# Pooled attention and a routed feed-forward in one program: another order of issue for the attention part, and the reordering of the second static block's columns moved behind the last attention unit

## The chip, the cores and the metric

The kernel runs on one core of one Trainium2 chip. The metric is the device time of one execution in microseconds (us). Of the kernel before, three runs took 790.5, 791.36 and 796.12 us (median 791.36). The engines are called by their short names: PE (TensorE: matmuls and transposes), DVE (VectorE), ACT (ScalarE), POOL (GpSimd), and SP, which here only starts transfers (DMA).

## The reference

Attention with keys and values that are averaged over groups of 8 rows, then a feed-forward layer in which each token goes through one of 8 experts. The token's choice can depend on its forerunner: where a local gate is closed, it keeps the expert of the token before.

```python
B, H, S, D = 8, 8, 576, 64            # pool = 8, so 72 pooled keys per head
k_p = k.reshape(B, H, 72, 8, D).mean(axis=3);  v_p = v.reshape(B, H, 72, 8, D).mean(axis=3)
attn = softmax(q @ k_p.T / sqrt(D));           x = (attn @ v_p), heads side by side: [B, S, 512]
for b, s:                              # E = 8 experts, F = 1024
    fresh = argmax(x[b, s] @ w_gate)
    e = fresh if s == 0 or sigmoid(x[b, s] @ w_local) < 0.5 else the e of s - 1
    out[b, s] = softmax(x[b, s] @ w_gate)[e] * (relu(x[b, s] @ w1[e]) @ w2[e])
```

## The kernel before

The program has three parts. **Attention** (0 to some 233 us of the span): the 8 batch entries go in pairs; a pair has five units of query rows, so there are 20 units (unit 5*pair + t; t = 4 is the last rows of both entries, "stacked"). **Static blocks**: after two pairs the most used expert is chosen, its weights are loaded, and two blocks of 256 of its tokens are run through it by code without branches. **Blocks**: a loop over a table that the kernel computes runs all the remaining tokens, 256 at a time, and changes experts as the table says.

Attention and static blocks are written as steps, and nothing but hand-written lists of step names (PLAN, PLAN_B, PLAN_C, lines 54 to 99) sets the order in which the steps are issued: `run(plan)` calls `do(name, n)` (line 758), which issues that step's instructions to the engines' queues. Each engine then works through its own queue in that order and waits, instruction by instruction, for what it needs; nothing overtakes. The names:

- `lv`, `lk`, `lq`: SP starts the load of a tile of values, keys, queries. `lc`, `pf`: loads of the gate weights and prefill of the token lists.
- values (prep_v, line 408): `vp` pools a tile (POOL, or DVE with `.d`), `vt` transposes it (PE), `vc` copies it (ACT), `vl` multiplies it by the gate weights (PE), `vd` puts that into the table `vaug` (DVE, line 436), `vm` (place_v, line 439) puts the pooled values into `vaug` (line 444; POOL, or DVE with `.d`). `kp` pools keys (DVE).
- a unit n: `sc` scores (PE), `mx` row maxima (DVE, line 490), `sb` subtract (DVE, line 493), `ex` exponentials (ACT), `T0` to `T2` transposes (PE, line 524) with their copies `T0c` to `T2c` (ACT, tile aT), `v0` to `v2` products with the values (PE, line 566) with their copies (ACT, tile osb), `fs` sums and gate logits (DVE, line 583 on), `fp` and `fd` the two halves of the output rows (POOL and DVE, line 603; `.p`: both on POOL) and their store (SP).
- a pair: `rA`, `rT0` to `rP` the routing of its tokens, a chain over DVE, PE and ACT; then nine times `s`: POOL scatters token numbers into the lists `ids`.
- the chosen expert: `ch`, `er` choose it; `w1`, `w2` (SP) load its weights, 4 tiles each; `p1`, `p2` split a tile into a high and a low part: a cast on ACT (tile w1h or w2h), then a subtraction on POOL (lines 213, 218).
- a static block n: `il` (line 257) loads its token numbers from `ids` (SP, line 259, four transfers); `ga` (line 262) sums them on DVE (lines 263, 264) and gathers the rows on POOL (two transfers, line 270); `XR` (line 279) puts the gathered rows' columns in another order: two copies on ACT (line 281); `X0`, `X1` transpose them (PE, line 288) and split them (ACT, DVE). `L1`, `h0`, `h1`, `L2` are the columns of its two matrix products: `h0` is line 337 (ACT) and 338 (DVE). Three PSUM tiles hp hold the columns of the first product.

```python
    elif op == "ga":
        xgs[n] = ld.tile([P, 2, D], F32, name="qt", bufs=4)
        rows_gather(n, xgs[n], 4 * S)
    elif op == "XR":
        xgs[n], src = ld.tile([P, 2, D], F32, name="qt", bufs=4), xgs[n]
        rows_order(src, xgs[n])
    elif op == "p1":
        split1(first1[n], n, nc.vector if arg else nc.gpsimd)

def split1(src, c, eng):
    nc.scalar.copy(out=W1[0][:, c, :], in_=src)
    eng.tensor_tensor(out=W1[1][:, c, :], in0=src, in1=W1[0][:, c, :].bitcast(F32), op=ALU.subtract)
```

Of the kernel before, what the change touches and what calls it, by code (L numbers as in the profile page):

```python
# [59 lines left out]
T1:1 lv:9 kp:6 lk:8 T1c:1 T2:1 v2:2 T2c:1 sc:3 v2c:2 lk:9 fs:2 v0:1 lq:7 mx:3 fp:2 v0c:1 v1:1 fd.p:2 sb:3 vp:8 v1c:1  # L60
v2:1 sc:4 v2c:1 ex:3 fs:1 vt:6 lq:8 vt:8 mx:4 fp:1 vc:6 vc:8 T0:3 sb:4 vm:8 fd:1 vm:6 T0c:3 T1:3 kp:7 vp:7 T1c:3
T2:3 vl:6 T2c:3 sc:5 vd:6 ex:4 lk:10 T0:4 mx:5 vp:9 lv:10 lv:11 lq:9 T0c:4 T1:4 vl:8 T1c:4 vt:7 vd:8 sb:5 vc:7 v0:3
vm:7 lv:12 kp:8 v0c:3 v1:3 ex:5 lk:11 v2:3 v1c:3 vl:7 v2c:3 v0:4 fs:3 v0c:4 v1:4 vd:7 fp:3 T0:5 v1c:4 fs:4 fd.p:3
T0c:5 T1:5 rA:0 fp:4 T1c:5 T2:5 sc:6 fd.p:4 T2c:5 vp:11 vt:9 lq:10 mx:6 vt:11 vc:9 vl:9 vc:11 vm:11 rT0:0 vm:9 vd:9
# [24 lines left out]
""")
# [1130 lines left out]
```

## Time and profile before

| | us |
|---|---|
| three runs | 790.5, 791.36, 796.12 |
| the profiled execution | 789.34 |
| its span, from the first to the last instruction | 786.9 |
| attention, up to the first product of a static block | 233.6 |
| static blocks and the first of the table's, up to about | 300 |
| busy: PE, DVE, ACT, POOL | 657.8, 450.9, 273.8, 437.8 |
| mean granted clock of PE, as a share of full speed | 0.899 |

The profiled execution is 2.0 us below the median of the three runs. Times in rows count from the span's start. In a timeline a row is a run of like instructions: start, busy time, engine, line, operation, output <- input, count, and in brackets the idle time in front of it and what ended that.

### The profile page before, as it was taken

What the parts mean: (1) busy time and instruction counts of PE and PEld (TensorE: products, weight loads), DVE (VectorE), ACT (ScalarE), POOL (GpSimd) and SP (SyncE); (2) the same over time, 40 slices, a digit from 0 to 9 for tenths busy, and PEclk for the clock granted to TensorE, in tenths of its full rate; (3) what the DMA queues carried; (4) which work ended last, traced back from release to release, by engine and by line L of the source; (5) the groups of instructions that cost most, each with busy time, mean ns of one, the idle gap of its engine ahead of it and who ended that gap; (6) DMA issues with size and microseconds to landing.
All of it is one profiled execution on the core that took longest, in us unless ns stands there. A gap on an engine that the chain in (4) does not pass through costs nothing. (4 is left out here: it accounts for less than half of the span.)

```text
span 786.9 us, 14972 instructions
## 1 busy us (share of the span) xinstructions
PE 657.8 (84%) x3588; PEld 545.8 (69%) x3589; DVE 450.9 (57%) x1058; ACT 273.8 (35%) x613; POOL 437.8 (56%) x659
## 2 busy tenths in 40 slices
PE   2878989966687999799999799789979996999980
PEld 2767878855685788577878676568868774877860
DVE  4696758797276635233478237387824386633450
ACT  1244434433543323122164125165512165321130
POOL 5156766573664543456546556556656556646443
PEclk9998779866798999899999899899989997999995
DMA  7897745452312162111116116225711146411110
GB/s 236 284 317 248 234 174 180 146 202 54 122 54 67 31 203 106 44 41 42 42 56 242 52 36 213 83 91 197 256 54 35 42 132 223 176 50 42 42 41 29
DMA packets 49377, 96.77 MB, mean 123 GB/s; under 512 B 22974, under 2 KB 22978, under 8 KB 49348
## 3 DMA queue, kind: packets, MB, share of 16 engines
q1 hardware_dynamic: 38820, 74.34, 28.1%
q0 software_dynamic: 10528, 22.08, 8.7%
q8 instruction: 14, 0.23, 0.1%
q14 instruction: 15, 0.12, 0.0%
HBM read 76.28 MB, written 22.21 MB: 125 GB/s over the span
## 5 line engine op out<-in xcount | busy, mean ns | idle before, releaser
L314 POOL DMA_INDIRECT kt<-x_rows,idk x168 | 180.1, 1072 | 49.7 <-issue 43.4
L330 PE MATMUL hp<-x,w1h 128*128 128x512 f32 x376 | 147.1, 426 | 11.7 <-ACT w1h L212 5.0
L351 PE MATMUL o_ps<-w2h,ht_h 128*128 128x512 f32 x312 | 123.9, 397 | 2.7 <-PEq L1140 1.0
L351 PE MATMUL o_ps<-w2l,ht_h 128*128 128x512 f32 x312 | 122.8, 394 | 0.0
L351 PE MATMUL o_ps<-w2h,ht_l 128*128 128x512 f32 x312 | 122.8, 394 | 0.0
L332 PE MATMUL hp<-x,w1l 128*128 128x256 f32 x376 | 112.4, 299 | 8.0 <-DVE w1l L213 3.1
L330 PEld LDWEIGHTS hp<-x,w1h 128*128 128x128 f32 x376 | 76.5, 204 | 32.5 <-issue 11.2
L338 DVE TENSOR_TENSOR hs<-hp,hs 128x256 f32<-128x256 f32 x94 | 39.2, 423 | 100.1 <-ACT hs L337 66.3
L337 ACT COPY hs<-hp 128x256 f32<-128x256 f32 x94 | 34.3, 367 | 165.3 <-PE hp L332 46.1
L332 PEld LDWEIGHTS hp<-x,w1l 128*128 128x128 f32 x376 | 76.8, 204 | 13.4 <-issue 12.7
L566 PE MATMUL op<-vaug,aT 128*128 128x148 f32 (+4 forms) x448 | 75.4, 346 | 4.1 <-ACT aT L376 4.0
L566 PEld LDWEIGHTS op<-vaug,aT 128*128 128x128 f32 (+1 forms) x448 | 69.3, 208 | 9.5 <-ACT aT L376 5.2
L351 PEld LDWEIGHTS o_ps<-w2h,ht_h 128*128 128x128 f32 x312 | 59.5, 191 | 16.9 <-issue 4.5
L342 ACT ACTIVATE ht_h<-hs 128x256 fp32r<-128x256 f32 x136 | 57.0, 419 | 35.4 <-DVE hs L338 21.3
L351 PEld LDWEIGHTS o_ps<-w2h,ht_l 128*128 128x128 f32 x312 | 59.3, 190 | 12.8 <-DVE ht_l L343 0.2
L351 PEld LDWEIGHTS o_ps<-w2l,ht_h 128*128 128x128 f32 x312 | 59.5, 191 | 11.7
L1065 DVE TENSOR_SCALAR ob<-o_ps,m_a 128x512 f32<-128x512 f32 x42 | 31.4, 749 | 59.1 <-PE hp L332 16.2
L343 DVE SCALAR_TENSOR_TENSOR ht_l<-hs,ht_h 128x256 fp32r<-128x256 f32 x136 | 57.0, 419 | 8.0 <-ACT ht_h L342 7.1
L1086 POOL TENSOR_TENSOR kt<-idk,zf 128x8 f32<-128x8 f32 x20 | 8.6, 432 | 90.4 <-DVE idk L305 86.5
L1076 POOL DMA_INDIRECT out<-ob,m_e x42 | 44.8, 1067 | 25.0 <-issue 25.0
L702 POOL DMA_INDIRECT ids<-pm,pos x36 | 35.5, 988 | 19.1 <-DVE pos L699 9.4
L323 ACT CAST x<-qt 128x512 fp32r<-128x512 f32 x40 | 22.8, 618 | 60.3 <-DVE qt L318 60.3
(265 smaller groups left out, 1199.5 us busy)
## 6 DMA issues: line engine op xcount, KB each, us to landing
raw<-in_moe_w SPq DMA_DIRECT2D x56, 512.0 KB
kk<-in_k SPq DMA_DIRECT2D x16, 576.0 KB
vt_in<-in_v SPq DMA_DIRECT2D x16, 512.0 KB
...
```

The costliest lines, as they stand in the source:

```text
L314: nc.gpsimd.indirect_dma_start(out=xk[:, j, :], out_offset=None, in_=x_pc[0:4 * rows], in_offset=bass.IndirectOffsetOnAxis(ap=idk[:, j:j + ...
L330: nc.tensor.matmul(out=ps, lhsT=W1[0][:, kk, f * P:(f + 1) * P], rhs=xt[:, kk].rearrange("p i n -> p (i n)"), start=(kk == 0), stop=False, ...
L332: nc.tensor.matmul(out=ps[:, 0:2 * P], lhsT=W1[1][:, kk, f * P:(f + 1) * P], rhs=xt[:, kk, 0, :], start=False, stop=(kk == KD - 1), skip_g ...
L337: nc.scalar.copy(out=hb[:, 0, :], in_=ps[:, 2 * P:])
L338: nc.vector.tensor_tensor(out=hb[:, 1, :], in0=ps[:, 0:2 * P], in1=hb[:, 0, :], op=ALU.add)
L342: nc.scalar.activation(out=ht[0][:, f, :], in_=hb, func=AF.Relu)
L343: nc.vector.scalar_tensor_tensor(out=ht[1][:, f, :], in0=hb, scalar=0.0, in1=ht[0][:, f, :].bitcast(F32), op0=ALU.max, op1=ALU.subtract)
L351: nc.tensor.matmul(out=to[h], lhsT=ht[i][:, kk, h * P:(h + 1) * P], rhs=W2[j][:, kk, :], start=(n == 0), stop=(n == 3 * KF - 1))
L566: nc.tensor.matmul(out=out, lhsT=lhs, rhs=rhs if len(out.shape) == 3 else rhs.rearrange("p s x -> p (s x)"), start=all(x[0] != n for x in ...
L702: nc.gpsimd.indirect_dma_start(out=ids[u % 4].rearrange("t m w -> (t m) w"), out_offset=bass.IndirectOffsetOnAxis(ap=pos[:, u:u + 1], axis=0),
L1065: nc.vector.tensor_scalar(out=ob[:, h, :], in0=o_ps[h], scalar1=m_a[:, h, 1:2], scalar2=None, op0=ALU.mult)
L1076: nc.gpsimd.indirect_dma_start(out=outv, out_offset=bass.IndirectOffsetOnAxis(ap=m_e[h][:, 0:1], axis=0), in_=ob[:, h, :], in_offset=None, ...
```

## The change

The list of steps of the attention part is replaced by another list of the same steps, and one step leaves it: `XR:1`, the reordering of the second static block's columns, which stood at the end of PLAN, now stands in PLAN_B behind `rO:3`, a late step of the last pair's routing, and ahead of `L1:4`, the fifth column of the first static block. A few steps change engine: DVE places values (`vm.d`) of tiles 3, 5, 8, 9, 14, 18, 19, 20, 21 and 22 where it was 0, 4, 16, 18, 19, 20 and 23 (16 instructions of line 444 where there were 12), and pools (`vp.d`) tiles 2 and 23 where it was 3. The loop and the products of the static blocks stay as they are. PLAN_C is the same. One line more in the list shifts all line numbers behind it by one (444 is 445 after, and so on). From the lists, of some 34 lines each:

```diff
@@ PLAN
...
-s:0 p1:3 T1:15 rA:2 T0c:15 sc:16 T1c:15 T2:15 vt:21 T2c:15 mx:16 s:0 vt:23 vc:21 vl:21 vc:23 rT0:2 s:0 vd:21 sb:16
-vl:23 fp:13 rT1:2 il:0 il:1 vd:23 ex:16 vm.d:23 fp:14 sc:17 fd:13 vm:21 fd:14 rS0:2 T0:16 rS1:2 ga:0 XR:0 T0c:16
...
+T0:14 s:0 v0c:13 sb:15 v1:13 T0c:14 il:0 il:1 p1:0 T1:14 vp.d:23 v2:13 T1c:14 v1c:13 vl:19 v2c:13 vt:21 vd:19 ex:15
...
@@ PLAN_B
 rA:3 L1:0 h0:0 h1:0 L1:1 h0:1 L1:2 rT0:3 rS0:3 h1:1 rT1:3 h0:2 rS1:3 h1:2 L1:3 rT2:3 rE:3 rS2:3 h0:3 h1:3 rL:3 rO:3
-L1:4 rR:3 ct:0 rV:3 rP:3 h0:4 h1:4 s:0 s:0 s:0 s:0 s:0 s:0 s:0 s:0 s:0 L1:5 tc:0 cn:0 i1:0 h0:5 h1:5
+XR:1 L1:4 rR:3 ct:0 rV:3 rP:3 h0:4 h1:4 s:0 s:0 s:0 s:0 s:0 s:0 s:0 s:0 s:0 L1:5 tc:0 cn:0 i1:0 h0:5 h1:5
...
```

**First place: the weight splits on POOL and the placing of values on DVE.** POOL's queue before, from the fourth of the second pair's nine scatters (L702) on; w1l and w2l are splits of weight tiles:

```order
L702 DMA ids3_67<-pm_1704,pos_1721 65536x2
L702 DMA ids0_64<-pm_1704,pos_1721 65536x2
L702 DMA ids1_65<-pm_1704,pos_1721 65536x2
L213 TENSOR_TENSOR w1l_154<-kt_1791,w1h_153 128x1024
L218 TENSOR_TENSOR w2l_156<-vt_in_1793,w2h_155 128x1024
L213 TENSOR_TENSOR w1l_154<-kt_1795,w1h_153 128x1024
L213 TENSOR_TENSOR w1l_154<-kt_1849,w1h_153 128x1024
L702 DMA ids2_66<-pm_1704,pos_1721 65536x2
L213 TENSOR_TENSOR w1l_154<-kt_1890,w1h_153 128x1024
L702 DMA ids3_67<-pm_1704,pos_1721 65536x2
L702 DMA ids0_64<-pm_1704,pos_1721 65536x2
```

After, from the sixth scatter on (lines are one higher; xs_1821 and xs_1947 are the output rows of units 12 and 13, vaug3<-vs_1896 places value tile 23):

```order
L703 DMA ids1_65<-pm_1660,pos_1677 65536x2
L604 TENSOR_TENSOR xs_1821<-osb_1688,rr_1793 128x512
L703 DMA ids2_66<-pm_1660,pos_1677 65536x2
L703 DMA ids3_67<-pm_1660,pos_1677 65536x2
L703 DMA ids0_64<-pm_1660,pos_1677 65536x2
L214 TENSOR_TENSOR w1l_154<-kt_1799,w1h_153 128x1024
L445 TENSOR_TENSOR vaug3_210<-vs_1896,mk_97 128x2x64
L604 TENSOR_TENSOR xs_1947<-osb_1856,rr_1917 128x512
L214 TENSOR_TENSOR w1l_154<-kt_1801,w1h_153 128x1024
L219 TENSOR_TENSOR w2l_156<-vt_in_1791,w2h_155 128x1024
L267 MEMSET qt_2027 128x1024
L271 DMA qt_2027<-x_rows_63,idr0_191 128x512 x2
```

All nine scatters now stand ahead of the first split, and the gather of the first static block (L271) stands between the third split and the last two of w1. DVE's queue before, where the values of tiles 20, 18 and 19 are placed (L444), up to the row maxima of unit 15:

```order
L436 TENSOR_TENSOR vaug2_209<-rt_1839,mk_97 128x2x9
L436 TENSOR_TENSOR vaug2_209<-rt_1839,mk_97 128x3x9
L444 TENSOR_TENSOR vaug2_209<-vs_1549,mk_97 128x2x64
L444 TENSOR_TENSOR vaug2_209<-vs_1448,mk_97 128x2x64
L444 TENSOR_TENSOR vaug2_209<-vs_1448,mk_97 128x3x64
L444 TENSOR_TENSOR vaug2_209<-vs_1558,mk_97 128x3x64 x2
L490 TENSOR_REDUCE mx_1883<-sp_1856 128x12
L490 TENSOR_REDUCE mx_1883<-sp_1856 128x4
```

After, from the last table entries in front of the same placing (L445) to the subtraction of unit 15:

```order
L437 TENSOR_TENSOR vaug2_209<-rt_1808,mk_97 128x3x9
L445 TENSOR_TENSOR vaug2_209<-vs_1593,mk_97 128x2x64
L445 TENSOR_TENSOR vaug2_209<-vs_1519,mk_97 128x2x64
L445 TENSOR_TENSOR vaug2_209<-vs_1519,mk_97 128x3x64
L437 TENSOR_TENSOR vaug2_209<-rt_1825,mk_97 128x2x9
L604 TENSOR_TENSOR xs_1821<-osb_1688,rr_1793 128x512
L445 TENSOR_TENSOR vaug2_209<-vs_1612,mk_97 128x3x64 x2
L491 TENSOR_REDUCE mx_1862<-sp_1829 128x12
L491 TENSOR_REDUCE mx_1862<-sp_1829 128x4
L494 TENSOR_TENSOR ap_1863<-sp_1829,mx_1862 128x864
L494 TENSOR_TENSOR ap_1863<-sp_1829,mx_1862 128x288
```

The same five placing instructions now have the table entries and output rows of unit 12 among them; in the step list no `p1` or `p2` stands ahead of them.

**Second place: the first reordering on ACT.** ACT's queue before, from the exponentials of unit 16 (at_1999) to the first exponentials of unit 17; brow is the third pair's routing, aT_2041 holds transposes of unit 16, osb_2110 products of unit 15, and L281 is `XR:0`:

```order
L508 ACTIVATE at_1999<-ap_1998 128x2x80
L508 ACTIVATE at_1999<-ap_1998 128x128
L648 COPY brow_2077<-tp_2067 2x256
L281 COPY qt_2090<-qt_2080 128x4x4x32 x2
L376 COPY aT_2041<-tp_2072 128x512
L376 COPY aT_2041<-tp_2094 128x512
L376 COPY aT_2041<-tp_2105 128x128
L376 COPY osb_2110<-op_2111 128x444
L508 ACTIVATE at_2101<-ap_2100 128x2x2x216
```

After, where L282 is `XR:0`, from the exponentials of unit 16 (at_1958) to the routing copies (brow) of the third pair; osb_2042 holds products of unit 15, aT_2018 transposes of unit 16, w1h is the cast of a weight tile:

```order
L509 ACTIVATE at_1958<-ap_1957 128x2x80
L509 ACTIVATE at_1958<-ap_1957 128x128
L213 CAST w1h_153<-kt_1941 128x1024
L377 COPY osb_2042<-op_2043 128x444
L213 CAST w1h_153<-kt_1992 128x1024
L377 COPY aT_2018<-tp_2066 128x512
L377 COPY osb_2042<-op_2074 128x444
L282 COPY qt_2091<-qt_2027 128x4x4x32 x2
L377 COPY osb_2042<-op_2094 128x2x148
L377 COPY aT_2018<-tp_2080 128x512
L649 COPY brow_2111<-tp_2099 2x256
L649 COPY brow_2131<-tp_2119 2x256
```

Between the gather's issue and `XR:0` ACT now has two casts of w1 tiles, two copies of products (osb) and one of transposes (aT), where `XR:0` stood right behind `ga:0` in the list.

**Third place: the second reordering on ACT.** ACT's queue before, from the copies of unit 19's transposes and products on; L281 is `XR:1`, the rows hs<-hp and ht_h<-hs belong to the first static block's columns:

```order
L376 COPY osb_2399<-op_2400 128x444
L376 COPY osb_2399<-op_2411 128x148
L281 COPY qt_2429<-qt_2419 128x4x4x32 x2
L337 COPY hs_2466<-hp0_2477 128x256
L342 ACTIVATE ht_h_2461<-hs_2466 128x256
L337 COPY hs_2466<-hp1_2478 128x256
L648 COPY brow_2543<-tp_2538 2x256
L342 ACTIVATE ht_h_2461<-hs_2466 128x256
```

After, from the high part of the first column (L343; unit 19's copies stand ahead of it) to the reordering (L282):

```order
L343 ACTIVATE ht_h_2455<-hs_2460 128x256
L338 COPY hs_2460<-hp1_2472 128x256
L649 COPY brow_2537<-tp_2532 2x256
L343 ACTIVATE ht_h_2455<-hs_2460 128x256
L338 COPY hs_2460<-hp2_2473 128x256
L649 COPY brow_2549<-tp_2542 2x256
L343 ACTIVATE ht_h_2455<-hs_2460 128x256
L649 COPY brow_2565<-tp_2562 2x128
L655 ACTIVATE pe_2568<-sh_2485 128x72
L338 COPY hs_2460<-hp0_2471 128x256
L343 ACTIVATE ht_h_2455<-hs_2460 128x256
L282 COPY qt_2586<-qt_2394 128x4x4x32 x2
```

The first four columns and the routing copies of the last pair (brow, pe) now stand ahead of the reordering; before, only unit 19's copies did.

On SP, before, the loads of all four w1 tiles stand ahead of the eight transfers of `il:0` and `il:1`, and three of w2 behind; after, two of w1 and one of w2 stand ahead, two of w1 and three of w2 behind.

## Rows read from the trace of the kernel before

**Rows 1.** Busy time by stage: PE, PEld, DVE, ACT, POOL; granted clock, DMA share, GB/s

```profile
0.00:110.00 110.00, 82.46 (x618) 71.99 (x619) 74.84 (x177) 37.39 (x93) 59.48 (x120) 0.89 0.76 252
...
150.00:200.00 50.00, 34.52 (x237) 27.90 (x236) 40.78 (x79) 17.00 (x36) 31.66 (x29) 0.67 0.38 125
200.00:233.60 33.60, 28.04 (x225) 25.62 (x225) 17.66 (x48) 18.70 (x41) 19.72 (x17) 0.83 0.20 72
233.60:300.00 66.40, 60.81 (x315) 49.52 (x312) 36.09 (x144) 21.41 (x56) 31.40 (x38) 0.95 0.35 113
300.00:786.90 486.90, 418.16 (x1919) 340.69 (x1917) 250.51 (x531) 160.78 (x341) 269.65 (x424) 0.92 0.28 92
```

**Rows 2.** DVE, row maxima (two instructions a unit, one if stacked) in two stretches

```profile
110.50:145.00 34.50, 5.01 (x8) 0.95 0.59 196
145.00:229.00 84.00, 8.52 (x12) 0.72 0.33 113
```

**Rows 3.** What PE waited for, 150 to 245 us: total us, times, longest

```profile
PE rt L428 <- DVE vaug L436: 7.1, 2, 4.6
PE tp L524 <- ACT aT L376: 6.6, 2, 5.9
PE tp L645 <- DVE ab L630: 3.3, 1, 3.3
...
PE hp L330 <- DVE hs L338: 1.7, 1, 1.7
```

**Rows 4.** Timeline of DVE, 149 to 240 us

```profile
163.22 10.90 DVE L444 TENSOR_TENSOR vaug<-vs,mk 128x128 f32<-128x128 f32 x5
174.05 1.41 DVE L490 TENSOR_REDUCE mx<-sp 128x12 f32<-128x864 f32 x2
...
180.45 1.69 DVE L622 TENSOR_TENSOR sh<-lg,ml 128x72 f32<-128x72 f32 x1
...
183.81 2.67 DVE L635 SCALAR_TENSOR_TENSOR ab<-bm,ac,nbm 128x2 f32<-128x2 f32 x1
...
216.80 2.12 DVE L586 TENSOR_TENSOR lgx<-osb,rr 128x144 f32<-128x144 f32 x1
```

**Rows 5.** Line 444, placing on DVE: ns min/median/max, first and last start

```profile
L444 DVE TENSOR_TENSOR vaug<-vs,mk x12: 268/376/7654, 18.1 to 190.4; 128x192 f32<-128x192 f32 x8, 128x128 f32<-128x128 f32 x4
```

**Rows 6.** Timeline of POOL, 0 to 235 us

```profile
163.95 2.36 POOL L213 TENSOR_TENSOR w1l<-kt,w1h 128x1024 fp32r<-128x1024 f32 x1
...
168.57 2.34 POOL L213 TENSOR_TENSOR w1l<-kt,w1h 128x1024 fp32r<-128x1024 f32 x1
...
197.14 1.09 POOL L270 DMA_INDIRECT qt<-x_rows,idr  x1 [9.32 <-DVE idr L264]
```

**Rows 7.** Timeline of PE, 150 to 245 us

```profile
164.24 2.84 PE L467 MATMUL sp<-kd,qt 64*128 64x72 f32 x24
...
203.15 0.48 PE L524 MATMUL tp<-ident,at 128*128 128x128 f32 x1 [5.93 <-ACT aT L376]
203.41 5.54 PE L566 MATMUL op<-vaug,aT 128*128 128x148 f32 x22
...
210.40 3.40 PE L566 MATMUL op<-vaug,aT 128*128 128x148 f32 x22
```

**Rows 8.** Timeline of ACT, 0 to 235 us

```profile
201.06 0.62 ACT L281 COPY qt<-qt 128x512 f32<-128x512 f32 x1 [5.79 <-DMA qt<-x_rows,idr]
```

**Rows 9.** Timeline of ACT, 229 to 246 us

```profile
241.97 0.62 ACT L281 COPY qt<-qt 128x512 f32<-128x512 f32 x1 [4.54 <-DMA qt<-x_rows,idr]
...
243.83 0.37 ACT L337 COPY hs<-hp 128x256 f32<-128x256 f32 x1
```

**Rows 10.** What SP waited for, 150 to 245 us

```profile
SPq L259 <- DMA ids<-pm,pos: 13.9, 1, 13.9
```

**Rows 11.** Timeline of SP, 145 to 262 us

```profile
185.88 6.54 SPq L259 DMA_DIRECT2D idn<-ids  x8
```

**Rows 12.** Line 444 on DVE, 150 to 233.6 us: count, busy us, mean ns

```profile
L444 DVE TENSOR_TENSOR vaug<-vs,mk 128x128 f32<-128x128 f32 (+1 forms) x6 | 11.2, 1915 | 0.0
```

More of the change, by code (lines that the diff above doesn't have):

```diff
@@ L60 @@
[L60 to L64, printed above, removed]
@@ new lines @@
+vc:2 vm:2 vp:1 lk:3 kp:1 lv:4 vt:1 lv:5 kp:2 vm:1 lk:4 sc:0 lk:5 vl:0 mx:0 lq:4 vc:1 vd:0 sb:0 vl:2 vd:2 ex:0 vl:1
+sc:2 vd:1 T0:0 mx:2 T0c:0 T1:0 vp:3 sb:2 v0:0 T1c:0 T2:0 kp:3 v1:0 v0c:0 T2c:0 lv:6 vt:3 v1c:0 v2:0 vm.d:3 vp:5
+vc:3 lk:6 vl:3 v2c:0 sc:1 vp:4 ex:2 vd:3 fs:0 vt:5 lq:5 lq:6 T0:2 mx:1 vc:5 fp:0 lv:7 lv:8 vt:4 vl:5 vm.d:5 vc:4
+vm:4 T0c:2 vd:5 kp:4 vl:4 fd.p:0 T1:2 vd:4 vp:6 v0:2 kp:5 lk:7 T1c:2 T2:2 v0c:2 v1:2 T2c:2 kp:6 lv:9 lk:8 v1c:2
+v2:2 sb:1 lk:9 vt:6 v2c:2 vm:6 fs:2 ex:1 sc:3 fp:2 vc:6 mx:3 lq:7 T0:1 vp:8 T1:1 T0c:1 sb:3 fd.p:2 v0:1 T1c:1 vp:7
@@ new lines @@
+T2:1 kp:7 v1:1 v0c:1 T2c:1 ex:3 v2:1 vp:9 lv:10 lv:11 lk:10 v1c:1 sc:4 v2c:1 T0:3 lq:8 fs:1 vl:6 lv:12 T0c:3 T1:3
+vd:6 vt:8 fp:1 mx:4 T1c:3 vm.d:8 vc:8 sb:4 T2:3 fd.p:1 vt:7 T2c:3 kp:8 vl:8 vc:7 sc:5 vm:7 ex:4 vd:8 kp:9 lk:11
+v0:3 lq:10 T0:4 v0c:3 mx:5 vp:11 lk:12 v1:3 T0c:4 vp:10 T1:4 sb:5 v1c:3 v2:3 T1c:4 vl:7 v2c:3 vt:9 vd:7 ex:5 vt:11
+fs:3 sc:6 lv:14 lv:13 vm:11 vc:11 vm.d:9 vc:9 fp:3 vl:11 lq:9 mx:6 T0:5 vt:10 fd.p:3 T0c:5 vd:11 v0:4 kp:10 vc:10
+vm:10 T1:5 v0c:4 sb:6 vp:12 lk:14 v1:4 T1c:5 kp:11 vl:9 v1c:4 T2:5 sc:7 T2c:5 ex:6 lv:15 fs:4 vt:12 lq:11 lk:13
@@ new lines @@
+T0:6 vd:9 fp:4 rA:0 vl:10 T0c:6 fd.p:4 vm:12 vc:12 T1:6 vp:14 T1c:6 T2:6 vp:13 T2c:6 lv:16 vd:10 v0:5 mx:7 rT0:0
+v0c:5 sb:7 lv:17 v1:5 rS0:0 vp:15 rT1:0 v1c:5 ex:7 v2:5 rS1:0 rT2:0 v2c:5 sc:8 lv:18 rS2:0 fs:5 rE:0 rL:0 lq:12
+mx:8 fp:5 T0:7 v0:6 rO:0 fd.p:5 T0c:7 sb:8 rR:0 v0c:6 vp:17 v1:6 rV:0 T1:7 v1c:6 rP:0 v2:6 T1c:7 T2:7 sc:9 v2c:6
+s:0 T2c:7 ex:8 fs:6 vl:12 vt:14 s:0 v0:7 mx:9 vc:14 fp:6 vd:12 T0:8 sb:9 v0c:7 s:0 v1:7 fd:6 T0c:8 vm.d:14 kp:12
+s:0 T1:8 v1c:7 v2:7 s:0 kp:13 T1c:8 lk:15 T2:8 vl:14 s:0 T2c:8 vt:13 v2c:7 sc:10 ex:9 fs:7 s:0 vc:13 v0:8 lq:13
@@ new lines @@
+lq:14 vd:14 mx:10 fp:7 T0:9 v0c:8 s:0 fd:7 v1:8 T0c:9 sb:10 s:0 T1:9 vl:13 v1c:8 v2:8 vm:13 T1c:9 vd:13 ex:10 kp:15
+vt:15 vt:17 sc:11 vm:17 v2c:8 vm:15 vc:15 fs:8 vc:17 v0:9 lq:15 vl:15 mx:11 v0c:9 v1:9 fp:8 T0:10 vd:15 v1c:9
+fd.p:8 sb:11 T0c:10 T1:10 fs:9 T1c:10 T2:10 sc:12 T2c:10 ex:11 rA:1 fp:9 fd.p:9 vl:17 vp:16 lq:16 T0:11 v0:10
+T0c:11 vd:17 lv:19 vt:16 mx:12 lv:20 v0c:10 v1:10 vm:16 vc:16 vl:16 vp:18 sb:12 v1c:10 v2:10 rT0:1 v2c:10 vd:16
+fs:10 rT1:1 lv:21 sc:13 rS0:1 fp:10 rS1:1 rT2:1 lq:17 fd.p:10 v0:11 rS2:1 vp:20 mx:13 T1:11 v0c:11 rE:1 vp:19 kp:14
@@ L89 @@
+X0c:0 fs:16 v0:17 T1c:17 fp:16 v0c:17 v1:17 rP:2 T2:17 fd:16 sc:19 v1c:17 s:0 T2c:17 ex:18 mx:19 v2:17 s:0 v2c:17
+s:0 T0:18 sb:19 fs:17 T0c:18 s:0 v0:18 fp:17 T1:18 s:0 v0c:18 fd:17 T2:18 T1c:18 s:0 T2c:18 ex:19 v1:18 s:0 T0:19
+v1c:18 s:0 v2:18 T0c:19 T1:19 s:0 v2c:18 ga:1 v0:19 T1c:19 fs:18 v0c:19 v1:19 fp:18 v1c:19 fs:19 fd.p:18 fp:19
+fd:19 ma:0
 """)
```

37 lines of the change are left out of this document (10 added, 27 removed).

## The prediction

> **What bounds the kernel now.** I read the busy times by stage first, then the row maxima, which mark when a unit begins, then PE's waits, and last the timelines around the places where PE waited. From 300 us on the loop keeps PE busy for 418.16 of 486.9 us [rows 1]. The edit does not touch it, so it is carried over as it is. Up to 110 us PE has 82.46 us of work and the DMA engines are busy for a share of 0.76: two limits close together. Between 150 and 200 us nothing is full: PE 34.52 of 50 us, DVE 40.78, POOL 31.66, and the granted clock is 0.67 of full, between the two levels of 1.2 and 2.4 GHz. So there the order of issue and the waits decide. The row maxima say it in units: four units begin in the 34.5 us from 110.5 on, 8.6 us each, at a mean clock of 0.95. In the 84 us from 145 on it is six more, 14 us each, at 0.72 [rows 2]. Most of the list's changes that can matter are in this slow stretch.
>
> PE's waits there are for table entries of the values (7.1 us in two), for transposes that ACT has to copy (6.6, of which 5.9 in one), for the routing (3.3), and at the first static block's columns for DVE (1.7) [rows 3]. I follow two of them back.
>
> The first goes to DVE. From 163.22 us on five placing instructions take 10.90 us [rows 4], though the median of line 444 is 0.376 us; its longest took 7.654 [rows 5]. The weight splits on POOL begin at 163.95, the first of four that follow each other; that at 168.57 is the third, each takes 2.3 us [rows 6]. DVE's slow stretch lies on POOL's. Behind it on DVE stand the row maxima of unit 15. PE's scores for them began at 164.24 and took 2.84 [rows 7], so they were there at 167.08; the maxima began at 174.05 [rows 4]: 7.0 us late for DVE alone.
>
> The second goes to ACT. `XR:0` waited 5.79 us for the gather from 195.3 to 201.06 [rows 8], and the copies of unit 16's transposes stood behind it; PE waited 5.93 and went on at 203.15 [rows 7]. The gather itself waited 9.32 us for the sums of the token numbers [rows 6], these for the eight small loads (6.54 us on SP's queue from 185.88 [rows 11]), and these for the scatters, 13.9 us [rows 10].
>
> **The change part by part.** The sum is made against the profiled 789.34 us.
>
> *Placing away from the splits.* After, the five placings stand ahead of the first split on DVE's and POOL's lists, and all nine scatters stand ahead of that split as well. If the queues run as they are written, the maxima of unit 15 need not wait for them: -7.0 us. What is late next is DVE's other work in front of them, table entries and output rows of one unit, which were there before too.
>
> *New neighbours of the splits.* The splits move some two units later. Beside them there are now the placings of tile 21 (two instructions). One instruction beside splits lost on average 10.90/5 - 0.376 = 1.8 us, so I take 2 x 1.8 = +3.6. The lower end is 0 (no overlap), the upper 2 x 7.654 = +15.3. The small operations of the routing and of the gate logits lose some in both versions: 1.69 us (line 622), 2.67 (635) and 2.12 (586) near splits [rows 4]; I count them equal.
>
> *`XR:0`.* On ACT two casts, two copies of products and one of transposes now stand between the gather's issue and the reordering. The wait of 5.79 us therefore has about one unit's work to hide in. The loads of the token numbers are issued earlier against the gather, since all scatters are ahead of them. I take 1.0 of PE's 5.93 us to be left, -4.9; the ends are 0 (the gather is as late against the new place) and -5.9.
>
> *`XR:1`.* Before, it stood at the head of ACT's queue when the first column's copy was due: it waited 4.54 us at 241.97, and the copy of the column came at 243.83 behind its two instructions [rows 9]. PE's price for that was 1.7 [rows 3], since the last pair's routing gave it other work. After, four columns are ahead of it, and the second block's transposes that need it come far behind. So -1.7, with 0 and -4.5 as ends.
>
> *Clock.* After its stall PE needed 5.54 us for 22 products of unit 16, and 3.40 for 22 of the next [rows 7]. With the stall gone these 2.1 are gone: -2.1. The upper end is nothing. The lower end is a PE that is never short of work: 34.52 us at 0.67 would be 34.52 x 0.67/0.91 = 25.4, thus -9.1, where 0.91 is an estimate between the 0.89 of the first and the 0.95 of the fifth row [rows 1].
>
> *The opening, up to 110 us.* Its list is written anew as well, pools and placings change engine: one more placing on DVE (seven for six, 0.4 us), beside 74.84 us of DVE work. PE's 82.46 and the DMA share of 0.76 stay, as the loads and products are the same. I take 0 and half a unit's 8.6 us to either side, 4.3.
>
> *Loads behind the token numbers.* Two w1 tiles and three of w2 are now issued behind the eight small loads on SP's queue; the casts on ACT that read them are in turn ahead of copies that PE needs. In the list there is a unit or more between such a load and its cast; I cost it at nothing and keep what it costs without that cover as a rival.
>
> Sum: -7.0 + 3.6 - 4.9 - 1.7 - 2.1 + 0 = -12.1, so 777.2 us for a run like the profiled one. That one lay 2.0 below the median of the three; the forecast of the median is 779 us. With the two large terms at their worse halves it is about 787, with the clock's and the column's ends about 771: its own range.
>
> **The rivals.**
> *A, the gather stays as late (0.16).* If the nine scatters and eight loads end no earlier against `XR:0` than before, the 5.93 us stall stays, and the slow products behind it: 779 + 4.9 + 2.1 = 786. For it: the chain from scatter to gather is 13.9 + 6.54 us on SP alone [rows 10, 11], and the gather waited 9.32 on POOL. Against it: the reordering has moved behind five more instructions.
>
> *B, weight tiles late (0.10).* The loads of two w1 tiles stand behind SP's wait for the scatters. That wait and the loads took 13.9 + 6.54 = 20.4 us; one unit of 8.6 between load and cast leaves 11.8 us in front of ACT's queue, two leave 3.2. The time would be 779 + 3.2 = 782 to 779 + 11.8 = 791. Against it: weights loaded in time before, and SP's wait need not be as long when all scatters come first.
>
> *C, slower: placing starves DVE (0.09).* DVE now has 16 placings instead of 12, nine instead of six behind the choice of the expert. Those six took 11.2 us, 1.915 each [rows 12]. If the new ones meet POOL's work (scatters, output rows, splits) as these did, all 16 at that mean make 30.6 us. Before, it was 11.2 and 6 x 0.376 = 2.3, together 13.5. That is 17.1 us more on DVE, which in the slow stretch is the fullest engine with 40.78 of 50 us. The stall of `XR:0` then hides behind DVE, and only -1.7 is left of the gains: 789.34 + 17.1 - 1.7 + 2.0 = 807. It decides from a mean of about 0.95 us per placing on, where the 16 cost the 13.5 + 1.7 us that they took before with the column's gain. Against it: seven of the 16 stand in the opening, where no split runs, and the median is 0.376.
>
> *D, PE's clock recovers (0.08).* If the stretch from 150 to 200 us gets as dense as that before it, the clock's term is -9.1 instead of -2.1: 772 us.
>
> *E, every small operation beside a split waits (0.05).* The routing chain of the third pair stands beside two w1 splits on POOL after. The rows show such operations slowed up to 2.67 us [rows 4], while the maxima of unit 15, which read PSUM, kept 1.41 us beside no split. If five operations of that chain lose the 1.8 us of a placing and PE waits for them, it is 779 + 9.0 = 788. Against it: lines 622 and 635 met a split before too. The Trainium skill, "GPSIMD Engine Reference", section "1. Specifications", says that GpSimd's SBUF interfaces are shared with VectorE, with contention for instructions in a 2-port mode or with two SBUF inputs; lines 444, 622 and 586 have two SBUF inputs, and the trace agrees with their 10.90, 1.69 and 2.12 us [rows 4]. By that rule this rival holds wherever such operations lie beside a split; without it the sum stays as it is.
>
> **How the numbers follow.** The forecast has 0.52, A 0.16, B 0.10, C 0.09, D 0.08, E 0.05. A measurement of this kernel tells about 1% from no change, 7.9 us: faster is below 783.4, slower above 799.3. The forecast's own range, 771 to 787, lies below 783.4 for about nine parts in ten, 0.47; with D's 0.08 and a fifth of B's it is 0.57. C is the 0.09 of slower. The rest, A, E, most of B and the forecast's upper tail, is 0.34 of no change. The range of 766 to 794 holds all but C, the worst of B with a poor opening, and a D with a better one.
>
> **What would show it.** Right: the five placings ahead of unit 15's maxima take less than 3 us together; `XR:0` on ACT waits less than 2 us and PE's wait for transposes of 5.9 us is gone; the column's copy follows unit 19's last copies with no wait for a gather; the first product of the static block comes before 222 us instead of 233.6; from there to the end it takes as long as before, some 553 us. Wrong: placings of several us beside splits elsewhere (C), a wait of ACT's casts for weight tiles (B), a gather that ends later than the reordering's place (A), or an opening whose unit 9 comes more than 4.3 us earlier or later.

## The result, and the profile after

The changed kernel takes 782.55 us (median of 11 runs, 773.77 to 788.06) where the kernel before, beside it, took 790.5 us. The ratio is 0.9858 with a 95% interval of 0.9823 to 0.9893. Of 790.5 us that is 11.2 us less, 8.5 to 14.0. The ratio is of the means of undisturbed runs, which leaves out the two longest of the changed kernel; with all runs the means lie 10.0 us apart and the medians 8.0. Forecast were 12.1. The profiled execution has a span of 779.5 us, 7.4 less than before. Its stages, with the columns of [rows 1]:

```profile
0.00:110.00 110.00, 81.70 (x628) 71.91 (x629) 76.07 (x184) 38.37 (x97) 55.79 (x113) 0.91 0.77 252
150.00:200.00 50.00, 38.35 (x298) 33.65 (x296) 40.66 (x91) 22.42 (x50) 34.33 (x30) 0.78 0.43 138
200.00:233.60 33.60, 29.19 (x217) 24.14 (x216) 23.14 (x65) 17.30 (x40) 21.97 (x18) 0.92 0.23 80
233.60:300.00 66.40, 62.95 (x316) 52.84 (x316) 39.18 (x141) 23.44 (x61) 27.11 (x38) 0.95 0.34 113
300.00:779.50 479.50, 408.97 (x1874) 333.92 (x1873) 244.31 (x518) 156.29 (x330) 266.83 (x418) 0.92 0.28 93
```

Up to 110 us the busy times are nearly the same. From 150 to 200 us PE got 38.35 us of work done where it was 34.52, at a granted clock of 0.78 for 0.67; from 200 to 233.6 the clock is 0.92 for 0.83 [rows 1]. DVE's busy time in the slow stretch is nearly the same, 40.66 for 40.78. The first product of a static block starts at 224.86 us, 8.8 earlier than before; from there to the end of the span it takes 554.6 us, where it was 553.3. So in these two executions the whole gain stands at the first product, as forecast.

DVE around the places of [rows 2, 4, 5, 12]: the placings, the row maxima (L491) of units 15, 16 and 17, and three operations of the third pair's routing; then line 445 as a group, from 150 to 228 us:

```profile
160.32 2.16 DVE L445 TENSOR_TENSOR vaug<-vs,mk 128x128 f32<-128x128 f32 x3
...
163.09 0.61 DVE L445 TENSOR_TENSOR vaug<-vs,mk 128x192 f32<-128x192 f32 x2
165.25 1.42 DVE L491 TENSOR_REDUCE mx<-sp 128x12 f32<-128x864 f32 x2 [1.55 <-PE sp L468]
...
173.27 3.15 DVE L445 TENSOR_TENSOR vaug<-vs,mk 128x128 f32<-128x128 f32 x2
176.34 1.41 DVE L491 TENSOR_REDUCE mx<-sp 128x12 f32<-128x864 f32 x2
...
185.21 0.22 DVE L622 TENSOR_REDUCE ml<-lg 128x9 f32<-128x72 f32 x1
185.46 2.68 DVE L623 TENSOR_TENSOR sh<-lg,ml 128x72 f32<-128x72 f32 x1
...
189.46 2.26 DVE L635 COPY ac<-ab 128x2 f32<-128x2 f32 x1
191.75 1.18 DVE L636 SCALAR_TENSOR_TENSOR ab<-bm,ac,nbm 128x2 f32<-128x2 f32 x1
...
192.98 1.41 DVE L491 TENSOR_REDUCE mx<-sp 128x12 f32<-128x864 f32 x2
```

```profile
L445 DVE TENSOR_TENSOR vaug<-vs,mk 128x192 f32<-128x192 f32 (+1 forms) x9 | 6.5, 768 | 0.0
```

The five placings take 2.16 + 0.61 = 2.8 us where they took 10.90, and unit 15's maxima follow when PE's scores are there. The two placings of tile 21 take 3.15. Nine placings have a mean of 0.768 us, not 1.915: DVE is not starved. Between unit 16 (176.34) and unit 17 (192.98) there are 16.6 us, though. In front of unit 17's maxima stands the routing chain of the third pair, lines 622 to 637, from 185.21 to 192.98: 7.8 us, with rows of 2.68, 2.26 and 1.18 us for operations that take 0.2 to 0.7 in the kernels below whose chain lies free. POOL at the same time, and then three rows of ACT:

```profile
182.69 1.09 POOL L271 DMA_INDIRECT qt<-x_rows,idr  x1 [3.17 <-DVE idr L265]
...
185.69 2.36 POOL L214 TENSOR_TENSOR w1l<-kt,w1h 128x1024 fp32r<-128x1024 f32 x1
189.32 2.37 POOL L214 TENSOR_TENSOR w1l<-kt,w1h 128x1024 fp32r<-128x1024 f32 x1 [1.28 <-ACT w1h L213]
191.64 1.27 POOL L383 TENSOR_TENSOR t<-vt_in 128x512 f32<-128x512 f32 x1
```

```profile
187.77 0.53 ACT L377 COPY osb<-op 128x444 f32<-128x444 f32 x1 [5.32 <-PE op L567]
...
190.18 1.14 ACT L282 COPY qt<-qt 128x512 f32<-128x512 f32 x2
...
227.58 0.37 ACT L338 COPY hs<-hp 128x256 f32<-128x256 f32 x1 [1.26 <-PE hp L333]
```

The two last w1 splits stand at 185.69 and 189.32, on the first two slow rows of the chain; on the third, at 191.75, POOL pools values (L383). The gather is issued at 182.69, 14.5 us earlier than in [rows 6], and `XR:0` on ACT (190.18) has no wait in its row, where it was 5.79 [rows 8]. PE's first product, and its waits:

```profile
224.86 0.50 PE L331 MATMUL hp<-x,w1h 128*128 128x512 f32 x1
```

```profile
PE sp L462 <- DVE ap L494: 7.5, 2, 4.2
...
PE op L567 <- ACT aT L377: 0.9, 2, 0.7
```

The wait of 5.9 us for aT of [rows 3, 7] is gone, and what is longest now are the waits of PE's scores (sp) for unit 16's and 17's subtraction on DVE (ap). Read so, the two profiles seem to confirm the sum: the placings no longer beside splits, the stall at `XR:0` gone, the routing chain the new loss. One execution of each can't say how much each was worth.

### The profile page after: what moved, and what is told of

It reads as the page before. It is cut to its first block, busy times and chain, and to the rows that moved or that the text cites. A ratio compares the mean times of both kernels' runs of the same rounds, so it can differ in the third digit from the quotient of the medians.

```text
span 779.5 us, 14984 instructions
## 1 busy us (share of the span) xinstructions
PE 654.1 (84%) x3588; PEld 545.5 (70%) x3589; DVE 457.9 (59%) x1062; ACT 271.4 (35%) x613; POOL 436.3 (56%) x653
## 5 line engine op out<-in xcount | busy, mean ns | idle before, releaser
L331 PE MATMUL hp<-x,w1h 128*128 128x512 f32 x376 | 146.3, 424 | 10.1 <-ACT w1h L213 4.8
L333 PE MATMUL hp<-x,w1l 128*128 128x256 f32 x376 | 111.9, 298 | 10.1 <-issue 4.6
L567 PE MATMUL op<-vaug,aT 128*128 128x148 f32 (+4 forms) x448 | 77.1, 335 | 2.8 <-ACT aT L377 1.2
L343 ACT ACTIVATE ht_h<-hs 128x256 fp32r<-128x256 f32 x136 | 57.0, 419 | 42.6 <-DVE hs L339 26.2
L352 PEld LDWEIGHTS o_ps<-w2h,ht_h 128*128 128x128 f32 x312 | 60.0, 192 | 16.6 <-issue 4.0
L344 DVE SCALAR_TENSOR_TENSOR ht_l<-hs,ht_h 128x256 fp32r<-128x256 f32 x136 | 59.4, 437 | 8.2 <-ACT ht_h L343 7.1
L383 POOL TENSOR_TENSOR t<-vt_in 128x512 f32<-128x512 f32 (+1 forms) x22 | 24.7, 1122 | 43.9 <-DMA vt_in<-in_v 43.4
```

The costliest lines, as they stand in the source:

```text
L331: nc.tensor.matmul(out=ps, lhsT=W1[0][:, kk, f * P:(f + 1) * P], rhs=xt[:, kk].rearrange("p i n -> p (i n)"), start=(kk == 0), stop=False, ...
L333: nc.tensor.matmul(out=ps[:, 0:2 * P], lhsT=W1[1][:, kk, f * P:(f + 1) * P], rhs=xt[:, kk, 0, :], start=False, stop=(kk == KD - 1), skip_g ...
L343: nc.scalar.activation(out=ht[0][:, f, :], in_=hb, func=AF.Relu)
L344: nc.vector.scalar_tensor_tensor(out=ht[1][:, f, :], in0=hb, scalar=0.0, in1=ht[0][:, f, :].bitcast(F32), op0=ALU.max, op1=ALU.subtract)
L352: nc.tensor.matmul(out=to[h], lhsT=ht[i][:, kk, h * P:(h + 1) * P], rhs=W2[j][:, kk, :], start=(n == 0), stop=(n == 3 * KF - 1))
L567: nc.tensor.matmul(out=out, lhsT=lhs, rhs=rhs if len(out.shape) == 3 else rhs.rearrange("p s x -> p (s x)"), start=all(x[0] != n for x in ...
```

## The experiments

The runs came in three groups on different chips; a chip's time may differ from another's, so ratios are against the kernel before on the same chip. The lists differ in length, and a line's number shifts with them: 443, 444 and 445 are the same line, as are 621, 622 and 623.

**One part at a time, in the list of before.** First the placings alone:

```diff
-vl:18 mx:14 vt:20 p1:0 w1:2 sb:14 vc:19 vd:18 sc:15 p2:0 vm.d:20 vm.d:18 vm.d:19 ex:14
+vl:18 vm.d:20 vm.d:18 vm.d:19 mx:14 vt:20 p1:0 w1:2 sb:14 vc:19 vd:18 sc:15 p2:0 ex:14
```

> The list of before; only the five placings of tiles 20, 18 and 19 on DVE are moved from behind the first splits to ahead of unit 14's row maxima. Theory of the sum: the 7 us that DVE lost beside the splits reach the end: maxima of unit 15 at about 167 us instead of 174.05, first product of the static block 7 us earlier than 233.64, ratio about 0.991. Rival (a fixed gather): the gather's chain over POOL's scatters and SP's loads does not move, unit 15 is earlier, but ACT's first reordering still goes on at about 201 us and waits 10 us or more; first product within 2 us of before, ratio 0.998 to 1.000.

Ratio 0.9996 (0.9957 to 1.0034). The placings took 1.29 us, unit 15's maxima came at 169.66 instead of 174.05, the first product at 230.68 instead of 233.64, and in time it was worth nothing that could be measured. PE waited 6.0 us for aT behind `XR:0`, and the gather held it until then. The fixed gather was right as to the time; its 10 us on ACT were 5.6.

Then `XR:1` alone:

```diff
-s:0 v1c:19 s:0 ga:1 XR:1 ma:0 fs:19
+s:0 v1c:19 s:0 ga:1 ma:0 fs:19
...
-rL:3 rO:3 L1:4
+rL:3 rO:3 XR:1 L1:4
```

> The list of before; only XR:1 moved from the end of PLAN to behind rO:3 in PLAN_B, as in the changed kernel. Theory of the sum: -1.7 us behind unit 19, attention itself unchanged, ratio 0.998. Rival 1: PE's other work hid the wait, 1.000. Rival 2: it is the main gain of the change, -4.5 us or more, 0.994 or lower.

Ratio 1.0017 (0.9980 to 1.0054), and from the first product (231.76) to the end of the span (784.8) 553.0 us, as before. The wait went from ACT's row (246.63, none), and PE had not needed it: rival 1. This kernel's attention is the one of before, instruction by instruction up to `XR:1`, so its profile says something else as well. DVE's placings and PE behind `XR:0` in it:

```profile
163.80 1.29 DVE L443 TENSOR_TENSOR vaug<-vs,mk 128x128 f32<-128x128 f32 x5
167.39 1.42 DVE L489 TENSOR_REDUCE mx<-sp 128x12 f32<-128x864 f32 x2 [2.31 <-PE sp L466]
```

```profile
PE tp L523 <- ACT aT L375: 10.4, 1, 10.4
```

The five placings took 1.29 us, and no split met them: the first split began at 166.94, behind a scatter. So the 10.90 us of [rows 4] do not belong to this order. And PE's stall is 10.4 us, not 5.93. A second profile of the kernel before itself was to settle it:

> The kernel before itself, one look. Theory (the 10.9 us of placing are an accident of one execution): the five placings of line 444 take less than 3 us and unit 15's maxima are not late for them, while the first reordering still waits 5 to 8 us for the gather. Rival (they belong to this order): 8 us or more again.

One run, one profile (792.85 us, span 790.5). Placings, POOL's first split and PE's stall:

```profile
164.80 2.14 DVE L444 TENSOR_TENSOR vaug<-vs,mk 128x128 f32<-128x128 f32 x5
168.73 1.42 DVE L490 TENSOR_REDUCE mx<-sp 128x12 f32<-128x864 f32 x2 [1.79 <-PE sp L467]
```

```profile
169.55 2.37 POOL L213 TENSOR_TENSOR w1l<-kt,w1h 128x1024 fp32r<-128x1024 f32 x1
...
194.35 1.08 POOL L270 DMA_INDIRECT qt<-x_rows,idr  x1 [5.21 <-DVE idr L264]
```

```profile
204.11 0.47 PE L524 MATMUL tp<-ident,at 128*128 128x128 f32 x1 [10.14 <-ACT aT L376]
```

2.14 us for the placings, unit 15 at 168.73, and 10.14 us of stall behind `XR:0`, the first product at 236.16. In this order the gather ends at much the same time whatever unit 15 does: in the three profiles (before, `XR:1` alone, the second of before) unit 15's maxima stand at 174.05, 167.39 and 168.73, 6.7 us apart, and the second copy of `XR:0` on ACT at 201.99, 200.76 and 202.95, 2.2 apart. Where the placings meet the splits, 7 us go there and the stall is shorter; where they don't, the stall takes them. It seems to take what else is late as well: with the placings alone it is 6.0 us although they are free, and there the routing chain took 7.0 us (some 4.4 in the other two) and PE waited 3.5 us for the values' table (vaug).

What ends the gather may be the weight loads that SP issues beside it. `XR:1` alone, then the changed kernel:

```profile
193.16 2.37 SPq L208 DMA_DIRECT2D vt_in<-in_moe_w  x3
```

```profile
196.17 1.93 SPq L210 DMA_DIRECT2D vt_in<-in_moe_w  x3
```

With `XR:1` alone the two parts of the gather were issued at 191.47 and 192.86 and copied at 197.05 and 200.76, 5.6 and 7.9 us later, while the DMA engines' busy share was 0.92 to 1.03 from 192 to 200 us. In the kernel before they were issued at 197.14 and 198.53, and it took 3.9 and 3.5 us. So an earlier issue brought little; that the loads are the reason is argued, not shown. In the changed kernel these loads stand 12 us or more behind the gather. No run moves them alone.

`XR:0` alone, and the three edits together:

```diff
-rS1:2 ga:0 XR:0 T0c:16
+rS1:2 ga:0 T0c:16
...
-vt:22 v2c:15 rT2:2
+vt:22 v2c:15 XR:0 rT2:2
```

> The list of before; only XR:0 moved some ten steps down, behind v2c:15. Theory of the sum: PE's wait of 5.93 us for unit 16's transposes and the slow products behind it go, first product 5 to 8 us earlier, ratio 0.990 to 0.994. Rival: the next thing in the list (scores or routing of the third pair) is as late, and the first product moves by less than 2 us, ratio 0.998 or more.

> The list of before with the three edits together (placings of tiles 20, 18, 19 ahead; XR:0 behind v2c:15; XR:1 in PLAN_B). Theory of the sum: 7.0 + 4.9 + 2.1 + 1.7 = 15.7 us less, ratio 0.980, lower than the whole change (0.986), because the new neighbours of the splits cost the whole change something that these three don't add. Rival (the other reordering of the list carries the gain): no more than half of that, ratio 0.990 or above.

`XR:0` alone: ratio 0.9931 (0.9890 to 0.9973), first product at 225.26 us; PE's longest wait between 190 and 210 us is 3.6 us, for ACT's copy of a values transpose (vT). All three: 0.9912 (0.9873 to 0.9951), first product 226.88. The two intervals lie on each other; the other two edits add nothing that can be measured, and the sum of 0.980 fell. The gain of 0.7% is the one step.

**What the whole change has more.** The changed kernel again, on the chip of the next three:

> The changed kernel itself, beside the others on one chip. Both theories: the ratio of 0.986 again within 0.004. Theory now (the gain is the first reordering, and the placings met the splits only in the one profiled execution): its five placings of tiles 20, 18, 19 again take less than 3 us, the gather is again some 12 us earlier than in the kernel before, and the chain of the third pair's routing lies beside two w1 splits again with unit 17's maxima some 16 us behind unit 16's.

Ratio 0.9839 (0.9794 to 0.9883). Placings 2.15 and 0.61 us, the gather issued at 180.04, unit 16 at 173.71, unit 17 at 190.33 and the first product at 222.06: the same picture. (On this chip the kernel before takes 744.12 us; see the last section.) With `XR:0` put back behind the gather:

```diff
-fs:14 vl:23 ga:0 fp:14
+fs:14 vl:23 ga:0 XR:0 fp:14
...
-mx:17 XR:0 v2:15
+mx:17 v2:15
```

> The changed kernel with XR:0 put back right behind ga:0 on ACT's list; the early gather stays. Theory L (the later place of XR:0 is what pays): ACT waits some 5 us for the gather at about 182 us, PE waits for unit 16's products or transposes behind it, first product 4 to 7 us later, ratio 0.992 to 0.995. Theory G (the gather being early is what pays, the place matters only while it is late): the wait on ACT lies in time in which ACT has nothing else to do (it waited 5.3 us for PE there), first product within 2 us of the changed kernel, ratio within 0.003 of it.

Ratio 0.9779 (0.9745 to 0.9813): faster than the changed kernel beside it (727.19 us for 731.4; the intervals just overlap), which neither theory had expected. ACT and DVE:

```profile
184.99 0.62 ACT L281 COPY qt<-qt 128x512 f32<-128x512 f32 x1 [4.86 <-POOL xs L603]
...
186.83 1.04 ACT L212 CAST w1h<-kt 128x1024 fp32r<-128x1024 f32 x1
...
188.19 1.05 ACT L212 CAST w1h<-kt 128x1024 fp32r<-128x1024 f32 x1
```

```profile
184.07 0.37 DVE L622 TENSOR_TENSOR sh<-lg,ml 128x72 f32<-128x72 f32 x1
...
185.76 0.17 DVE L634 COPY ac<-ab 128x2 f32<-128x2 f32 x1
185.96 0.22 DVE L635 SCALAR_TENSOR_TENSOR ab<-bm,ac,nbm 128x2 f32<-128x2 f32 x1
...
186.23 1.41 DVE L490 TENSOR_REDUCE mx<-sp 128x12 f32<-128x864 f32 x2
```

ACT waits 4.86 us for the gather again, and PE did not feel it: theory G, the gather is early enough that the wait lies where ACT would have waited for PE anyhow (it waited 3.08 and 5.32 us for it in the two profiles of the changed kernel). A side effect shows where the gain may come from. The casts of the two last w1 tiles stand behind `XR:0` on ACT, so POOL's splits came later, and the routing chain ran free: 0.37 us for line 622 where it was 2.67, unit 17's maxima at 186.23 for 190.33, the first product at 219.37 for 222.06. The profiled execution doesn't keep that to the end: it is the second longest of the eight, 731.48 us, and the changed kernel's was 731.34.

The other way round, the gather early in the list of before:

```diff
-vl:18 mx:14 vt:20 p1:0 w1:2
+vl:18 mx:14 vt:20 s:0 s:0 s:0 p1:0 w1:2
...
-mx:15 p1:1 w1:3 lq:19 T0:14
+mx:15 p1:1 w1:3 lq:19 il:0 il:1 T0:14
...
-T2c:15 mx:16 s:0 vt:23
+T2c:15 mx:16 ga:0 vt:23
```

(the three `s:0` and the old `il` and `ga:0` behind it are gone from their places)

> The kernel before with the second pair's last three scatters ahead of the first split, il:0 and il:1 behind lq:19 and ga:0 behind unit 16's maxima; XR:0 stays where it is, right behind rS1:2. Theory G: the gather lands at about 190 us instead of 201, ACT's first reordering waits less than 1 us, first product 5 to 8 us earlier than 233.6, ratio about 0.992 as with XR:0 alone moved. Theory L: something else holds the gather or PE in its place, first product within 2 us, ratio 0.998 or more.

Ratio 0.9929 (0.9897 to 0.9962), but not by the theory's way, and it decides nothing between G and L; what brought it is open. The gather was issued at 194.42, no earlier than in the list of before (191.47 to 197.14), because the three scatters pushed the splits down, the splits held the buffers of the next w1 tiles (SP waited 10.1 us for one), and ACT stood for one of them:

```profile
182.36 1.04 ACT L212 CAST w1h<-kt 128x1024 fp32r<-128x1024 f32 x1 [10.20 <-DMA kt<-in_moe_w]
```

```profile
188.00 2.35 POOL L213 TENSOR_TENSOR w1l<-kt,w1h 128x1024 fp32r<-128x1024 f32 x1 [2.16 <-ACT w1h L212]
...
194.42 1.06 POOL L270 DMA_INDIRECT qt<-x_rows,idr  x1 [2.85 <-DVE vaug L436]
```

That 10.20 us is the wait of rival B (weight tiles late), which this kernel has and the changed one has not.

**The routing chain.** Two ways to free it. First the chain behind unit 17's maxima:

```diff
-p1:2 v0:15 rA:2 T0:16
+p1:2 v0:15 T0:16
...
-v2:15 rT0:2 fd:14 v2c:15 sb:17 T1c:16 rT1:2
+v2:15 fd:14 v2c:15 sb:17 rA:2 T1c:16 rT0:2 rT1:2
```

> The changed kernel with rA:2 behind sb:17 and rT0:2 behind T1c:16, so that the third pair's routing chain on DVE stands behind unit 17's maxima. Theory (the chain beside two splits takes 7.8 us on DVE and is what is late next): unit 17's maxima at about 185 us instead of 193, first product 3 to 7 us earlier, ratio 0.977 to 0.982. Rival: the routing itself is due (its rows, the lists and the last pair's chain wait for it), first product within 2 us or later, ratio 0.984 or more.

Ratio 0.9846 (0.9812 to 0.9880), as the changed kernel's. Unit 17's maxima came at 183.42, 6.9 us earlier, and unit 18's at 202.09, as in the changed kernel (201.97): the chain's later steps on PE were due then, and PE waited 3.5 us for the chain's line 630. The rival was right. Then the splits behind unit 17's maxima and the chain in its place:

```diff
-vd:23 p1:2 v0:15 rA:2 T0:16 v0c:15 p1:3 v1:15
+vd:23 v0:15 rA:2 T0:16 v0c:15 v1:15
...
-mx:17 XR:0
+mx:17 p1:2 p1:3 XR:0
```

> The changed kernel with the last two w1 splits (p1:2, p1:3) moved down behind unit 17's maxima, XR:0 in its place of the changed kernel. Theory (the splits on POOL slow the routing chain on DVE that lies beside them): the chain from line 622 to 637 takes less than 4 us instead of 7.8, unit 17's maxima come 4 us earlier, first product 2 to 4 us earlier, ratio about 0.978 as with XR:0 put back. Rival (putting XR:0 back gained for another reason): ratio as the changed kernel's, 0.984.

Ratio 0.9785 (0.9719 to 0.9851): 767.94 us where the kernel before took 786.74 on that chip. DVE and POOL:

```profile
179.32 0.22 DVE L621 TENSOR_REDUCE ml<-lg 128x9 f32<-128x72 f32 x1
179.57 0.23 DVE L622 TENSOR_TENSOR sh<-lg,ml 128x72 f32<-128x72 f32 x1
...
181.33 0.55 DVE L634 COPY ac<-ab 128x2 f32<-128x2 f32 x1
181.92 0.65 DVE L635 SCALAR_TENSOR_TENSOR ab<-bm,ac,nbm 128x2 f32<-128x2 f32 x1
...
182.62 1.41 DVE L490 TENSOR_REDUCE mx<-sp 128x12 f32<-128x864 f32 x2
```

```profile
186.10 4.65 POOL L213 TENSOR_TENSOR w1l<-kt,w1h 128x1024 fp32r<-128x1024 f32 x2 [3.56 <-ACT w1h L212]
```

The chain takes 3.3 us, unit 17's maxima stand at 182.62, and the first product at 217.26. Of the 7.6 us by which the first product is earlier than in the changed kernel, 4.8 stand at unit 16 already (171.54): unit 13 was 1.0 earlier, and tile 21's placings, between the first two splits in this execution and not beside one, took 0.98 us. From unit 16 to unit 17 it is 11.1 us instead of 16.6. The interval overlaps the changed kernel's, so this run alone proves little.

**Tile 21's placings.** Two last runs move them behind unit 16's subtraction, one with `XR:0` back, one with the splits late, each with this edit more:

```diff
-w1:2 vm.d:21 vc:23
+w1:2 vc:23
...
-T1:15 sb:16 v0c:14
+T1:15 sb:16 vm.d:21 v0c:14
```

> The changed kernel with XR:0 right behind ga:0 and the two placings of tile 21 on DVE behind unit 16's subtraction instead of ahead of its maxima. Theory (the 3.1 us of placing beside the first split hold unit 16 and PE behind it, which waited 4.2 us for that subtraction): unit 16's maxima 2 to 3 us earlier, ratio 0.974 to 0.977. Rival: something else is due at the same time, ratio 0.978 as without it.

> The changed kernel with p1:2 and p1:3 behind unit 17's maxima and tile 21's placings behind unit 16's subtraction; XR:0 in its place of the changed kernel. Theory: both gains add, ratio 0.974 to 0.977. Rival: the later casts of the weights come into the way of unit 17's or 18's copies on ACT, ratio 0.980 or more.

Ratios 0.9784 (0.9734 to 0.9833) and 0.9797 (0.9746 to 0.9848): nothing beside 0.9779 and 0.9785. In the second, unit 16's maxima came at 169.94, 1.6 us earlier than with the splits late alone, and the first product at 217.55 for 217.26. The theory fell; tile 21's placings had stood beside the second split, not the first as the expectation has it. The four kernels whose routing chain lies free of the splits (2.4 to 3.3 us) have 0.9779, 0.9785, 0.9784 and 0.9797; the three runs of kernels where it does not (the changed kernel twice, and the late routing) 0.9858, 0.9839 and 0.9846. Single intervals of the two sets overlap; no ratio of one lies among the other's. So some 0.6% goes with that meeting, and by these ratios `XR:0` back or the splits late is faster than both kernels of this study. Two things weaken it: on the chip of the last three the changed kernel was not run, and each of the four edits moves the casts on ACT together with the splits, so the splits' part alone is argued from the rows.

## Why the prediction was right or wrong

The executions of the two lists side by side, the starts of a unit's row maxima and of the first product; up to unit 13, all of the upper seven run the list of before, all of the lower seven the list after (us from the span's start):

| execution | unit 9 | unit 13 | unit 15 | first product |
|---|---|---|---|---|
| before | 110.68 | 144.99 | 174.05 | 233.64 |
| before, second profile | 112.61 | 149.27 | 168.73 | 236.16 |
| `XR:1` alone | 109.02 | 147.99 | 167.39 | 231.76 |
| placings alone | 107.67 | 148.88 | 169.66 | 230.68 |
| `XR:0` alone | 107.71 | 149.45 | 169.32 | 225.26 |
| the three | 107.12 | 148.81 | 170.01 | 226.88 |
| gather early | 115.67 | 152.31 | 169.95 | 230.99 |
| after | 106.40 | 144.64 | 165.25 | 224.86 |
| after, second profile | 105.45 | 143.29 | 162.36 | 222.06 |
| `XR:0` back | 106.31 | 143.07 | 163.27 | 219.37 |
| routing late | 105.72 | 143.08 | 163.20 | 224.61 |
| splits late | 104.81 | 143.62 | 162.18 | 217.26 |
| `XR:0` back, tile 21 | 106.39 | 145.38 | 165.36 | 220.52 |
| splits late, tile 21 | 104.95 | 142.40 | 161.62 | 217.55 |

The total was right: 12.1 us forecast, 11.2 measured. The parts that make it up were not: a gain that wasn't there stood in the sum, gains and a loss that were there did not, and that they nearly cancel is luck.

*Placing away from the splits, -7.0: the step failed.* It was read from a stretch of one execution, and the same order ran the same five placings in 1.29, 1.33 and 2.14 us in three others. Where the 7 us did occur they were cover for the gather; moving the placings alone gave a ratio of 0.9996. "Late for DVE alone" was true of unit 15 in that execution, but the next thing late was the gather, and the sum counted both.

*`XR:0`, -4.9, and the clock behind it, -2.1: right in kind, too small.* The stall is 10.1 and 10.4 us in the two profiles where little else is late, and moving the step alone brought 0.69% of 788.04, 5.4 us, with the first product some 8.6 us earlier than the mean of the first three rows. The prediction took the later place of the step as the reason. In the changed kernel it is the earlier gather that does it, as the run with `XR:0` put back shows: the place alone costs nothing there. In the list of before, where the gather is late, the place is what pays. What makes the gather early, its own place or that of the w2 loads, is open.

*New neighbours of the splits, +3.6: wrong place.* Tile 21's placings took 3.15 us, 2.4 more than two medians, and moving them away gave nothing. The routing chain, counted as equal in both versions, was the loss. In the profiled kernel before it took 6.7 us, from its first row to unit 16's maxima:

```profile
180.19 0.23 DVE L621 TENSOR_REDUCE ml<-lg 128x9 f32<-128x72 f32 x1
...
186.87 1.41 DVE L490 TENSOR_REDUCE mx<-sp 128x12 f32<-128x864 f32 x2
```

```profile
179.62 2.43 POOL L213 TENSOR_TENSOR w1l<-kt,w1h 128x1024 fp32r<-128x1024 f32 x1 [4.90 <-DVE rr L584]
...
184.49 1.61 POOL L603 TENSOR_TENSOR xs<-osb,rr 128x512 f32<-128x512 f32 x2
```

That, too, was one execution: in the seven upper rows of the table it took 6.7 and 7.0 us in two and 4.4 to 5.2 in five. In the changed kernel it takes 7.8 in both profiles, and 2.4 to 3.3 free; freeing it went with a ratio of 0.979 instead of 0.985. The prediction also misread a row: the 2.67 us of line 635 [rows 4] stand beside output rows on POOL (184.49), not beside a split. Rival E was this mechanism, at 9 us and a chance of 0.05; what was there to be had by avoiding it is 0.006 of 788, some 5 us. The rule that the prediction cites there from the Trainium skill, "GPSIMD Engine Reference", section "1. Specifications", agrees with lines 623 (2.68 us, 0.23 to 0.37 free) and 636 (1.18 us, 0.22 to 0.67 free), which have two SBUF inputs. Line 635, a copy with one input, was slow too (2.26 us, 0.17 to 0.55 free), and no run tells whether that is the page's other case, a 2-port mode, or something else.

*The opening, 0: the step failed.* It was put at nothing because loads and products are the same, with 4.3 us to either side. Unit 9 has a mean of 110.1 us over the upper seven rows and 105.7 over the lower seven, without overlap; unit 13 has 148.8 and 143.6, 5 us earlier. One row hides that: the profiled execution of before is the earliest of its seven at unit 13 (144.99), and lies among the lower ones. Not all of the 5 us arrive. With `XR:0` alone the first product comes at 225.26, in the two profiles of the changed kernel at 224.86 and 222.06, and only where the routing chain is free at 217.26 to 220.52. So most of the opening's gain seems to be lost again at the chain. Which edit of the opening does it was not tried.

*`XR:1`, -1.7: wrong.* The wait left ACT's row, but the time stayed; the routing of the last pair had covered all of it.

*Loads behind the token numbers, 0: right.* Rival B occurred in small at most: in the second profile of the changed kernel one cast waited 2.13 us for its weight tile (181.01), and PE then waited for nothing on ACT for 2 us or more. Rivals A and C did not occur: 0.768 us per placing is below its point of 0.95. Rival D's clock came half way, to 0.78.

Of the signs that the prediction named, the placings' 2.8 us, `XR:0` without a wait, the column's copy and the 553 us behind it were seen, and the first product before 222 us was not, by 3 us. Unit 9 stands 4.28 us earlier, on the edge of the 4.3 that it named as a sign of being wrong.
